# Moving five more transposes from TensorE to DMA in a sparse attention with a dense mixture of experts

## The chip, the cores and the metric

The kernel runs on one core of a Trainium2 chip. The metric is device time in microseconds (us), the median of several runs. A profile of one execution gives the time of every instruction on the engines: TensorE (PE in the profile, PEld its weight loads), VectorE (DVE), ScalarE (ACT), GpSimd (POOL) and SyncE (SP), which only issues DMAs.

## The reference, cut to what matters

Attention comes first: 4 batches of 8 heads, 768 positions, 64 features. Each query sees the keys nearer than 16 positions and 24 block summaries (the maximum of each block of 32 keys, the mean of its values). The result goes into a mixture of 8 experts in which every token takes every expert, weighted by a matrix P that eight rounds of row and column normalization make (a Sinkhorn iteration).

```python
    k_sum = k.reshape(B, H, nb, block, D).max(axis=3)
    v_sum = v.reshape(B, H, nb, block, D).mean(axis=3)
    scores_l = scale * np.matmul(q, k.transpose(0, 1, 3, 2))
    mask_l = np.abs(pos[:, None] - pos[None, :]) < window
    scores_s = scale * np.einsum('bhsd,bhnd->bhsn', q, k_sum)
    scores_s = scores_s + np.log(block)
    # ... softmax over the masked near scores and the summaries together, then
    v_all = np.concatenate([v, v_sum], axis=2)
    return np.matmul(a, v_all).astype(np.float32)
    # ... the experts: x is 3072 x 512, F = 1024
    P = np.exp(logits)
    for _ in range(8):
        P /= P.sum(1, keepdims=True) + 1e-09
        P /= P.sum(0, keepdims=True) + 1e-09
        P *= N / E
    for e in range(E):
        h = np.maximum(x @ w1[e], 0.0)
        ye = h @ w2[e]
        out += P[:, e:e + 1] * ye
```

## The kernel before

The heads are worked on in 16 pairs, four pairs to a batch (`PB` = 4, `NP` = 16). The first four pairs are done in halves; pairs 4 to 15 whole. Every operation of attention and of the first expert is a unit with an engine, an estimated cost, the units it waits for, a priority, and a `lag` by which its result is taken to reach those who wait for it later. A planner written in Python orders the units when the kernel is built, by these estimates. So each engine's queue is fixed before it runs, and the order of one unit changes the order of others. What runs on the chip still waits by semaphores.

Queries and keys arrive with positions along the partitions and are needed with features there. Up to pair 11 TensorE transposes them, six 128x128 blocks each, into a PSUM bank, and ScalarE or VectorE copies them out. From pair 12 on a DMA transposes them:

```python
        def tr(i, z, tag):
            st = at.pop(("st", i, z))
            t = at["t", i, z] = bank(tag, "tkq", BF16)
            for g in range(G):
                if i < PB:
                    for j in range(2):
                        nc.tensor.transpose(t[64 * j:64 * j + 64, g * 128:(g + 1) * 128],
                                            st[:, j, g, :], ident)
                else:
                    nc.tensor.transpose(t[:, g * 128:(g + 1) * 128],
                                        st[:, g, :, :].rearrange("p j d -> p (j d)"), ident)

        def tr_dma(i, z):
            r, st = i % NB, at.pop(("st", i, z))
            nc.sync.dma_start_transpose(out=(kT[r][:], qT[r][:, W:W + S])[z].rearrange("c (g t) -> c g t", g=G),
                                        in_=st[:].rearrange("p g j d -> p (g j d)"))

        def x_dma(i):
            nc.sync.dma_start_transpose(
                out=xT[:, i % PB, i // PB * S:(i // PB + 1) * S].rearrange("c (g t) -> c g t", g=G),
                in_=at.pop(("xs", i, 0))[:].rearrange("p g j d -> p (g j d)"))
# ... (cut)
        def pair_start(i, prio):
            o = i - NB
            war_k = [U.get(("S", o, 0)), U.get(("S", o, 1)), U.get(("km", o))]
            war_q = war_k[:2] + [U.get(("ss", o, 0)), U.get(("ss", o, 1))]
            tag = "m" if i < PB else "a"
            for z in range(2 if i >= PB else 1):
                if i >= 12:
                    U["tr", i, z] = U["kT", i, z] = add("SP", 1.25, lambda z=z: tr_dma(i, z),
                                                        [U["kq"[z], i]] + (war_k, war_q)[z], prio, lag=5.0)
                    continue
                buf = Buffer(tag)
                U["tr", i, z] = add("PE", 0.4, lambda z=z: tr(i, z, tag),
                                    [U["kq"[z], i], U["ident"]] + (war_k, war_q)[z]
                                    + [U["tr", i, 0] if z else U.get(("S", i - 1, 1 if i > PB else 0))],
                                    prio, opens=[buf])
                U["kT", i, z] = add({"ACT": 0.8} if z == 0 else {"ACT": 0.8, "DVE": 0.95},
                                    0, lambda z=z: tr_out(U["kT", i, z].on, i, z), [U["tr", i, z]], prio,
                                    uses=[buf])
```

The four `kT` and `qT` tiles are used in turn (`NB` = 4), so pair 12's transpose overwrites pair 8's. Attention's output goes the same two ways into `xT`, the input of the experts:

```python
        def to_xT(i, h=None):
            t = at.pop(("xs", i, h or 0))
            tx = at["tx", i, h] = bank("a", "tx", FP16)
            for g in range(G if h is None else HG):
                nc.tensor.transpose(tx[:, g * 128:(g + 1) * 128],
                                    t[:, g, :, :].rearrange("p j d -> p (j d)"), ident16)
# ... (cut, in pair_whole)
            if 10 <= i < 15:
                U["xt", i] = U["x", i] = add("SP", 1.25, lambda: x_dma(i), [U["no", i, 0], U["no", i, 1]], prio,
                                             lag=4.5)
            else:
                buf = Buffer("a")
                U["xt", i] = add("PE", 0.35, lambda: to_xT(i), [U["no", i, 0], U["no", i, 1]], prio, opens=[buf])
                U["x", i] = add({"ACT": 0.8, "DVE": 0.9}, 0, lambda: x_out(U["x", i].on, i), [U["xt", i]], prio,
                                uses=[buf])
```

The small copies of neighbouring values (`near_values`, into `Ve`) are issued on the same SyncE queue. GpSimd issues the loads of queries, keys, values and weights. A small copy of one element on GpSimd makes the loads of expert 1's weights wait for the last query transposes:

```python
        def hold():
            for r in range(12 % NB, NB):
                nc.gpsimd.tensor_copy(out=held[0:1, 0:1], in_=qT[r][0:1, W:W + 1])

        last[0] = add("POOL", 0.3, hold, [last[0]] + [U["kT", i, 1] for i in range(12, NP)])
        for i in range(4):
            load(("w1n", i), lambda i=i: load_w1(1, i), 0.85, 1.3)
        load("w2n", lambda: load_w2(1), 0.85, 5.0)
```

The first expert's products (`hidden0` at line 200 and `project0` at line 210) are planned between the pieces of attention, with lower priority, and go on after attention has ended. When the last logits are there, the eight rounds of normalization begin, each of six units on three engines (the loop in `bridge`):

```python
                for eng, us, fn, o, w in (("DVE", 0.62, rows, (), ()), ("POOL", 0.7, by_rows, (), ()),
                                          ("DVE", 0.48, columns, (), ()), ("PE", 0.12, totals, [buf], ()),
                                          ("DVE", 0.2, inverse, (), [buf]), ("POOL", 0.7, by_columns, (), ())):
                    step = add(eng, us, fn, [step], -50.0, opens=o, uses=w, lag=(1.2 if n else 2.0) if fn is columns else 0.0)
```

`totals` is a small matmul by which TensorE sums the columns over the partitions; the profile calls its output "sink". Experts 1 to 7 are computed by a scheme with seven block products in place of eight (the Strassen-Winograd scheme; lines 907 and 913), in a fixed order. The last four pairs of output blocks, A to D, end the kernel. B and D use other PSUM banks (`spare`), and their last sums are split:

```python
            def ahead():
                between(out_acc[:, tb, 0:DH], out_acc[:, tb, 0:DH], out_acc[:, tb, DH:DM])

            def y_half():
                s3 = fast.tile([128, DH], FP32, tag="y3", name="y3", bufs=1)
                nc.scalar.activation(out=s3[:], in_=at(3), func=AF.Copy, scale=P_sb[:, ta, e:e + 1])
                add(tb, 1, 2)
                store(tb, slice(DH, DM))
                nc.vector.scalar_tensor_tensor(
                    out=out_acc[:, tb, 0:DH], in0=at(2), scalar=P_sb[:, tb, 0:1],
                    in1=out_acc[:, tb, 0:DH], op0=ALU.mult, op1=ALU.add)
                nc.gpsimd.tensor_tensor(out=out_acc[:, ta, DH:DM], in0=out_acc[:, ta, DH:DM], in1=s3[:], op=ALU.add)

            def x_half():
                add(ta, 0, 0)
                store(ta, eng=nc.scalar)
                nc.vector.scalar_tensor_tensor(
                    out=out_acc[:, tb, 0:DH], in0=at(1), scalar=P_sb[:, tb, 0:1],
                    in1=out_acc[:, tb, 0:DH], op0=ALU.mult, op1=ALU.subtract)
                store(tb, slice(0, DH))
# ... (cut)
        A, B, C, D = last
        for d, nm in ((A, "q1"), (g, "r21"), (A, "c1"), (q, "ya"), (q, "yb"), (g, "s4"), (B, "q1"), (B, "c1"),
                      (A, "q5"), (A, "v5"), (D, "q1"), (D, "c1"), (B, "q5"), (B, "v5"), (C, "q1"), (C, "c1"),
                      (A, "q6"), (A, "v6"), (D, "q5"), (D, "v5"), (B, "q6"), (B, "v6"), (q, "fin"), (B, "ahead"), (D, "ahead"),
                      (C, "q5"), (C, "v5"), (D, "q6"), (D, "v6")):
            d[nm]()
        for n, d in enumerate(last):
            if n == 1:
                C["q6"]()
                C["v6"]()
            for nm in (("q2", "q4", "q3", "q7", "ya", "yb", "fin"),
                       ("q7", "q3", "y_half", "q2", "q4", "x_half"))[n % 2]:
                d[nm]()
```

`between` is a subtraction, on GpSimd for these four; `add` is one VectorE operation that multiplies a PSUM block by a column of P and adds it to `out_acc`.

## Time and profile before

| | |
|---|---|
| time, median of 3 runs | 677.02 us (675.16 to 677.29) |
| profiled execution, span from first to last instruction | 673.4 us |
| PE busy | 663.9 us (99%), 5111 matmuls |
| PEld busy | 434.8 us (65%) |
| DVE busy | 580.2 us (86%) |
| ACT busy | 402.5 us (60%) |
| POOL busy | 131.5 us (20%) |
| mean TensorE clock granted | 0.999 of full |
| chain that ended last | PE 93%, DVE 4%, DMA, POOL and issue 1% each |

The span is that of one execution, so it differs from the median. Matmuls overlap in TensorE's pipeline: their shown durations add up to more than the time they take, and the distance from one start to the next is the cost. An arrow `<-` in a line of the timeline separates what is written from what is read; in brackets stands the engine's idle time just before, and what ended it. Idle time of an engine that isn't the bottleneck costs nothing. The stages are: start-up to about 20 us, attention mixed with the first expert to about 123 us, the rest of the first expert with the normalization and the first groups of expert 1 to 168.8 us, experts 1 to 7 to the end.

### The profile page before, as it was taken

The page shows a single profiled execution, that of the slowest core. Times are in us where ns is not written, and L with a number is a line of the kernel's source. Part 1 is how long each engine was busy: PE and PEld are TensorE (multiplying, and loading weights), DVE is VectorE, ACT ScalarE, POOL GpSimd, SP SyncE. Part 2 cuts the span into 40 slices and gives each one's busy share as a digit, 9 for nine tenths or more (in the row PEclk, how much of TensorE's full clock was granted, in tenths as well). Part 3 has the DMA queues.
Part 4 walks back from the last instruction along what each step waited for, and adds up shares of the span by engine and source line. Part 5 has one row for each costly group of instructions (what it writes and reads, how often), then busy time and mean ns, then how long its engine had stood idle before and what let it go on. Part 6 is the DMA issues. An engine that isn't in the chain of part 4 may idle for free.

```text
span 673.4 us, 13531 instructions
## 1 busy us (share of the span) xinstructions
PE 663.9 (99%) x5111; PEld 434.8 (65%) x5111; DVE 580.2 (86%) x1433; ACT 402.5 (60%) x783; POOL 131.5 (20%) x177
## 2 busy tenths in 40 slices
PE   8999999999999999999999999999999999999996
PEld 4666655555666666666666666666666666666665
DVE  6878889777799988998899988998899889998885
ACT  4777776565777765555655565555555555556552
POOL 8599622122101010201010010101020101100001
PEclk9999999999999999999999999999999999999999
DMA  9999959000513060311422050405031141201224
GB/s 115 190 147 145 151 85 172 2 1 1 79 11 37 1 79 1 36 14 21 59 22 28 1 78 9 40 1 79 1 33 17 20 60 20 30 0 48 82 91 158
DMA packets 124018, 36.46 MB, mean 54 GB/s; under 512 B 110384, under 2 KB 121136, under 8 KB 123952
## 3 DMA queue, kind: packets, MB, share of 16 engines
q0 software_dynamic: 104672, 26.22, 41.8%
q1 hardware_dynamic: 18464, 8.83, 5.6%
q8 instruction: 40, 0.66, 0.4%
q10 hardware_dynamic: 816, 0.54, 0.2%
q14 instruction: 26, 0.21, 0.1%
HBM read 52.45 MB, written 6.29 MB: 87 GB/s over the span
## 4 chain that ended last, share of the span: by engine, by line
PE 93%; DVE 4%; DMA 1%; POOL 1%; issue 1%; ACT 0%; DVEq 0%; ACTq 0%
PE xy L913 36%; PE pg L907 16%; PE pa L907 11%; PE pb L907 11%; PE hps L200 6%; PE yps L210 6%; PE sg L334 1%; DMA kst<-in_k_dram 1%; DVE hf L857 1%; PE tkq L305 1%; PE vs L342 1%; PE av L406 1%; PE av L412 1%; PE ss L430 1%; PE tx L517 0%
## 5 line engine op out<-in xcount | busy, mean ns | idle before, releaser
L913 PEld LDWEIGHTS <-hf 128*128 128x128 f16 x2352 | 230.1, 98 | 95.6 <-issue 0.5
L913 PE MATMUL xy<-w,hf 128*128 128x256 f16 x1312 | 183.4, 273 | 0.0
L913 PE MATMUL xy<-ws,hf 128*128 128x256 f16 x984 | 147.6, 273 | 0.1
L191 ACT ACTIVATE hf<-pg 128x512 f16<-128x512 f32 x84 | 50.2, 597 | 150.8 <-PE pg L907 150.8
L1049 DVE SCALAR_TENSOR_TENSOR out_acc<-xy,P_sb,out_acc 128x512 f32<-128x512 f32 x164 | 115.1, 744 | 2.1 <-PE xy L913 2.1
L854 DVE TENSOR_TENSOR hf<-hf 128x512 f16<-128x512 f16 x252 | 100.3, 424 | 8.8
L907 PE MATMUL pa<-xT,w 128*128 128x512 f16 x336 | 99.9, 379 | 0.0
L907 PEld LDWEIGHTS <-w 128*128 128x128 f16 x672 | 65.8, 98 | 44.4 <-issue 1.1
L857 DVE TENSOR_TENSOR hf<-pb,c 128x512 f16<-128x512 f32 x84 | 58.1, 692 | 38.5 <-PE pb L907 32.4
L176 POOL DMA_DIRECT2D w<-in_moe_w_dram x56 | 41.7, 754 | 220.6 <-PE pg L907 192.0
L907 PEld LDWEIGHTS <-ws 128*128 128x128 f16 x504 | 49.3, 98 | 25.3
L941 ACT COPY c<-pg 128x512 f32<-128x512 f32 x84 | 49.2, 586 | 22.4 <-PE pg L907 22.4
L857 DVE TENSOR_TENSOR hf<-pg,c 128x512 f16<-128x512 f32 x84 | 57.2, 681 | 0.8 <-PE pg L907 0.8
L926 ACT COPY pg<-pa 128x512 f32<-128x512 f32 x84 | 47.9, 570 | 4.8
L191 ACT ACTIVATE hf<-pa 128x512 f16<-128x512 f32 x84 | 50.6, 602 | 0.0
L907 PE MATMUL pg<-xTs,w 128*128 128x512 f16 x168 | 50.0, 379 | 0.2
L907 PE MATMUL pg<-xT,w 128*128 128x512 f16 x168 | 50.0, 379 | 0.1
L907 PE MATMUL pb<-xT,ws 128*128 128x512 f16 x168 | 50.0, 379 | 0.0
L907 PE MATMUL pb<-xTs,ws 128*128 128x512 f16 x168 | 50.0, 379 | 0.0
L907 PE MATMUL pg<-xTs,ws 128*128 128x512 f16 x168 | 50.0, 379 | 0.0
L934 ACT COPY c<-pb 128x512 f32<-128x512 f32 x84 | 49.8, 592 | 0.0
L200 PE MATMUL hps<-xT,w 128*128 128x384 f16 x256 | 48.6, 326 | 0.0
(141 smaller groups left out, 820.1 us busy)
## 6 DMA issues: line engine op xcount, KB each, us to landing
w<-in_moe_w_dram POOLq DMA_DIRECT2D x8, 1024.0 KB, 8.9
w<-in_moe_w_dram POOLq DMA_DIRECT2D x56, 128.0 KB, 3.5
out_dram<-out_acc SPq DMA_DIRECT2D x20, 256.0 KB, 2.0
qst<-in_q_dram POOLq DMA_DIRECT2D x32, 96.0 KB, 5.7
vx<-in_v_dram POOLq DMA_DIRECT2D x16, 192.0 KB, 6.5
kst<-in_k_dram POOLq DMA_DIRECT2D x24, 96.0 KB, 5.9
w<-in_moe_w_dram POOLq DMA_DIRECT2D x2, 512.0 KB, 8.6
kst<-in_k_dram POOLq DMA_DIRECT2D x4, 192.0 KB, 5.1
```

The costliest lines, as they stand in the source:

```text
L176: nc.gpsimd.dma_start(out=t[:, :, h, :], in_=moe_w1[e].rearrange("(dk p) f -> p dk f", p=128)[:, :, f:f + 128])
L191: nc.scalar.activation(out=out, in_=in_, func=AF.Relu, bias=0.0, scale=1.0)
L200: nc.tensor.matmul(hp[:, 0:n], lhsT=w1s[e][:, dk, 128 * f:128 * (f + 1)], rhs=xT[:, dk, t0:t0 + n], start=(dk == 0), stop=(dk == KD - 1))
L210: nc.tensor.matmul(yp[:], lhsT=h[:, f, c * 128:(c + 1) * 128], rhs=w2s[e][:, f, :], start=(f == 0), stop=(f == KF - 1))
L854: nc.vector.tensor_tensor(out=out, in0=in0, in1=in1, op=ALU.subtract)
L857: nc.vector.tensor_tensor(out=out, in0=in0, in1=in1, op=ALU.add)
L907: nc.tensor.matmul(bank[:], lhsT=w[:, dk, :], rhs=x[:, dk, :], start=start and dk == 0, stop=dk == KH - 1, skip_group_check=True)
L913: nc.tensor.matmul(bank, lhsT=a(f)[:, 128 * c:128 * (c + 1)], rhs=w[:, f, :], start=start and f == 0, stop=f == FH - 1, skip_group_check=True)
L926: nc.scalar.copy(out=B["g"][:], in_=B["a"][:])
L934: nc.scalar.copy(out=B["c5"][:], in_=B["b"][:])
L941: nc.scalar.copy(out=B["c2"][:], in_=B["g"][:])
L1049: nc.vector.scalar_tensor_tensor(out=acc, in0=src, scalar=P_sb[:, t, e:e + 1], in1=acc, op0=ALU.mult, op1=ALU.add)
```

## The change

The keys and queries of pairs 10 and 11 are transposed by DMA in place of TensorE, and so is the output of pair 9. The purpose is to take these transposes off TensorE's queue and the copies behind them off ScalarE and VectorE. The hold on the weight loads follows: it now names all transposes from pair 10 on in the plan, and reads the two tiles written last (those of pairs 14 and 15). The result of the first round's column totals is taken to come 1.4 us later in the plan, so that other work comes ahead of the reciprocal that waits for it in VectorE's queue. And the end of the output pairs B and D is rebuilt: ScalarE's scaling, GpSimd's addition and the subtraction done in advance go; one VectorE sum takes the place of two operations, and the subtraction comes after the second half's sum.

```diff
--- before.py
+++ after.py
@@ -640,7 +640,7 @@
             war_q = war_k[:2] + [U.get(("ss", o, 0)), U.get(("ss", o, 1))]
             tag = "m" if i < PB else "a"
             for z in range(2 if i >= PB else 1):
-                if i >= 12:
+                if i >= 10:
                     U["tr", i, z] = U["kT", i, z] = add("SP", 1.25, lambda z=z: tr_dma(i, z),
                                                         [U["kq"[z], i]] + (war_k, war_q)[z], prio, lag=5.0)
                     continue
@@ -725,7 +725,7 @@
                                    prio, opens=[buf])
                 U["no", i, h] = add("DVE", 0.68, lambda h=h: normalize(i, h),
                                     [U["A", i, h], U.get(("xt", i - 2))], prio, uses=[buf])
-            if 10 <= i < 15:
+            if 9 <= i < 15:
                 U["xt", i] = U["x", i] = add("SP", 1.25, lambda: x_dma(i), [U["no", i, 0], U["no", i, 1]], prio,
                                              lag=4.5)
             else:
@@ -816,10 +816,10 @@
                 expert0(b * S, xs)
                 expert0(b * S + HS, xs)
         def hold():
-            for r in range(12 % NB, NB):
+            for r in range(10 % NB, NB):
                 nc.gpsimd.tensor_copy(out=held[0:1, 0:1], in_=qT[r][0:1, W:W + 1])
 
-        last[0] = add("POOL", 0.3, hold, [last[0]] + [U["kT", i, 1] for i in range(12, NP)])
+        last[0] = add("POOL", 0.3, hold, [last[0]] + [U["kT", i, 1] for i in range(10, NP)])
         for i in range(4):
             load(("w1n", i), lambda i=i: load_w1(1, i), 0.85, 1.3)
         load("w2n", lambda: load_w2(1), 0.85, 5.0)
@@ -1068,18 +1068,11 @@
                     between(out_acc[:, tb, 0:DH], out_acc[:, tb, DH:DM], out_acc[:, tb, 0:DH])
                     store(tb)
 
-            def ahead():
-                between(out_acc[:, tb, 0:DH], out_acc[:, tb, 0:DH], out_acc[:, tb, DH:DM])
-
             def y_half():
-                s3 = fast.tile([128, DH], FP32, tag="y3", name="y3", bufs=1)
-                nc.scalar.activation(out=s3[:], in_=at(3), func=AF.Copy, scale=P_sb[:, ta, e:e + 1])
                 add(tb, 1, 2)
                 store(tb, slice(DH, DM))
-                nc.vector.scalar_tensor_tensor(
-                    out=out_acc[:, tb, 0:DH], in0=at(2), scalar=P_sb[:, tb, 0:1],
-                    in1=out_acc[:, tb, 0:DH], op0=ALU.mult, op1=ALU.add)
-                nc.gpsimd.tensor_tensor(out=out_acc[:, ta, DH:DM], in0=out_acc[:, ta, DH:DM], in1=s3[:], op=ALU.add)
+                between(out_acc[:, tb, 0:DH], out_acc[:, tb, 0:DH], out_acc[:, tb, DH:DM])
+                add(ta, 1, 3)
 
             def x_half():
                 add(ta, 0, 0)
@@ -1089,7 +1082,7 @@
                     in1=out_acc[:, tb, 0:DH], op0=ALU.mult, op1=ALU.subtract)
                 store(tb, slice(0, DH))
 
-            return {f.__name__: f for f in (scale0, q1, c1, q5, v5, q6, v6, q2, q7, q3, q4, ya, yb, fin, ahead, y_half, x_half)}
+            return {f.__name__: f for f in (scale0, q1, c1, q5, v5, q6, v6, q2, q7, q3, q4, ya, yb, fin, y_half, x_half)}
 
         def bridge():
             t = [fps.tile([128, 512], FP32, tag="g", name="allg", bufs=2) for _ in range(2)]
@@ -1129,7 +1122,7 @@
                 for eng, us, fn, o, w in (("DVE", 0.62, rows, (), ()), ("POOL", 0.7, by_rows, (), ()),
                                           ("DVE", 0.48, columns, (), ()), ("PE", 0.12, totals, [buf], ()),
                                           ("DVE", 0.2, inverse, (), [buf]), ("POOL", 0.7, by_columns, (), ())):
-                    step = add(eng, us, fn, [step], -50.0, opens=o, uses=w, lag=(1.2 if n else 2.0) if fn is columns else 0.0)
+                    step = add(eng, us, fn, [step], -50.0, opens=o, uses=w, lag=(1.2 if n else 2.0) if fn is columns else (0.0 if n else 1.4) if fn is totals else 0.0)
 
             X, Wt = {}, {}
             for j in range(2):
@@ -1251,7 +1244,7 @@
         A, B, C, D = last
         for d, nm in ((A, "q1"), (g, "r21"), (A, "c1"), (q, "ya"), (q, "yb"), (g, "s4"), (B, "q1"), (B, "c1"),
                       (A, "q5"), (A, "v5"), (D, "q1"), (D, "c1"), (B, "q5"), (B, "v5"), (C, "q1"), (C, "c1"),
-                      (A, "q6"), (A, "v6"), (D, "q5"), (D, "v5"), (B, "q6"), (B, "v6"), (q, "fin"), (B, "ahead"), (D, "ahead"),
+                      (A, "q6"), (A, "v6"), (D, "q5"), (D, "v5"), (B, "q6"), (B, "v6"), (q, "fin"),
                       (C, "q5"), (C, "v5"), (D, "q6"), (D, "v6")):
             d[nm]()
         for n, d in enumerate(last):
```

## The prediction

> **What bounds the kernel now.** I read the page's slices first, then the list of who waited for whom on TensorE, then the timeline around the places that the change touches. Of the slices of the page (40 slices of 16.8 us; digits are busy tenths):
>
> ```profile
> PE   8999999999999999999999999999999999999996
> DVE  6878889777799988998899988998899889998885
> DMA  9999959000513060311422050405031141201224
> ```
>
> TensorE is at nine tenths or more in every slice but the first and the last; the DMA engines are full in the first 67 us, while attention loads its queries, keys and values, and light afterwards. VectorE is high but has gaps. The list of waits says how little TensorE ever stands still (line, what it waited for: total us, times, longest):
>
> ```profile
> PE sink L1117 <- DVE csum_sb L1112: 0.8, 1, 0.8
> PE ss L430 <- DVE xT L196: 0.5, 1, 0.5
> ```
>
> The other three entries of that list lie in the start-up (1.0, 0.8 and 0.6 us). The chain of work that ended last is 93% TensorE. So the stage from about 20 to 169 us, in which attention is mixed with the first expert's products, lasts as long as TensorE's queue is: the expert's products (lines 200 and 210) are there as filling until 168.8 us, and an instruction taken out of TensorE's queue before that moves everything behind it forward. Work taken from ScalarE or VectorE moves nothing by itself.
>
> The timeline shows what the instructions in question cost (start, duration; the answers' "x6" are six merged instructions):
>
> ```profile
> 76.44 0.50 PE L305 MATMUL tkq<-ident,kst 128*128 128x128 bf16 x6
> 76.78 0.50 PE L305 MATMUL tkq<-ident,qst 128*128 128x128 bf16 x6
> 77.03 0.79 ACT L196 COPY kT<-tkq 128x768 bf16<-128x768 bf16 x1
> 77.20 0.53 PE L342 MATMUL vs<-vx,m_blk 128*64 128x128 bf16 x6
> 77.37 0.56 DVE L196 COPY qT<-tkq 128x768 bf16<-128x768 bf16 x1
> ...
> 81.22 0.50 PE L517 MATMUL tx<-ident,xs 128*128 128x128 f16 x6
> 81.65 0.38 PE L334 MATMUL sg<-qT,kT 64*128 64x160 bf16 x6
> 81.97 0.51 PE L305 MATMUL tkq<-ident,kst 128*128 128x128 bf16 x6
> 82.31 0.50 PE L305 MATMUL tkq<-ident,qst 128*128 128x128 bf16 x6
> 82.65 1.89 PE L210 MATMUL yps<-w,h 128*128 128x512 f16 x8
> ```
>
> These are the last transposes on TensorE for queries and keys (pair 10 at 76.44, pair 11 at 81.97) and the one for pair 9's output (81.22). A duration of 0.50 us contains the pipeline's run-out; what a block takes of the queue is the distance between starts.
>
> **What the Trainium skill says.** "Trace Analysis", section "Identifying the Most-Contended Engine", warns that the busy share of matmuls doesn't tell how near TensorE is to its limit because they are pipelined. Agreed here: six transposes show 0.50 us and take 0.34 (76.44 to 76.78), so I count starts. "VectorE: DVE Perf Modes", "The three transpose paths", has TensorE's transpose end in PSUM, so that a copy follows, and the crossbar DMA's end in SBUF; the trace shows the copies (0.79 us on ScalarE, 0.56 on VectorE). It gives 390 ns for one transpose on TensorE; back to back the trace has 57 (0.34 / 6), and the measurement decides. "DMA: Bandwidth & Descriptors", "Issuing engines are not separate DMA queues", says that DMAs from all queues interleave on the same 16 engines: the transposes added at 60 to 80 us share them with the loads. The table of DMA issues has (KB were not recorded; the number is us to landing)
>
> ```profile
> xT<-xs SPq DMA_TRANSPOSE x5, 4.9
> kT<-kst SPq DMA_TRANSPOSE x4, 5.2
> qT<-qst SPq DMA_TRANSPOSE x4, 3.6
> ```
>
> all after 76 us; beside full loads they may take longer, which no run of before shows.
>
> **The change part by part.**
>
> Transposes. Removed from TensorE: 4 blocks for queries and keys (pairs 10 and 11) and one for an output (pair 9), 30 transposes. Pair 10: 77.20 - 76.44 = 0.76 us. Pair 11: 82.65 - 81.97 = 0.68. Pair 9's output: 81.65 - 81.22 = 0.43. Sum 1.87 us of TensorE's queue, all of it on the path by the argument above. The floor, without the gaps ahead of the next block, is 30 x 57 ns = 1.71 us. Removed too: 2 copies of 0.79 us from ScalarE and 3 of 0.56 from VectorE (3.3 us together), beside other work, so worth nothing in themselves; they help the softmax chain, and free PSUM banks of the ring "a", which five blocks no longer take.
>
> Added: 5 DMA transposes on SyncE's queue, about 1.25 us of issue each (median 1.21 to 1.28 in the trace), 6.3 us in all, between about 60 and 88 us. That queue has room there: between 61.6 and 66.2 and between 68.7 and 73.0 us it issues nothing. Pair 10's keys and queries are issued for loading at 51.8 and 53.5 us and land about 5.8 us later (kst's median), pair 11's at 56.2 and 57.8; the ring entries they overwrite (pairs 6 and 7) are last read by about 62.7 us. So the transposes can be issued from 60 to 65 us, and even with 6 us to landing are done by 75, while pair 10's scores start only at 79.8. Pair 9's output is normalized by 80.7; by DMA it lands near 87, and its logits come after pair 11's output, which landed about 104. No wait follows from either.
>
> Weight loads. Before, GpSimd is held by the last query transpose until 98.0 us, then issues the loads for expert 1. The last transpose is still pair 15's, which waits for pair 11's scores; hence about the same moment, or up to 2 us earlier. First use is at 124.1 us, the last issue at 104.3 plus 8.9 to landing makes 113.2. About 11 us of slack: no effect.
>
> Column totals. TensorE stood 0.78 us before the first totals:
>
> ```profile
> 125.30 0.48 DVE L1112 TENSOR_REDUCE csum_sb<-P_sb 128x8 f32<-128x192 f32 x1
> 125.93 0.36 PE L1117 MATMUL sink<-csum_sb,col_en 128*128 128x8 f32 x2 [0.78 <-DVE csum_sb L1112]
> 128.04 0.20 DVE L1120 RECIPROCAL crec_sb<-sink 128x8 f32<-128x8 f32 x1
> ```
>
> A lag in the planner delays those who wait for a unit. The new 1.4 us is put on the totals, so it moves not them but the reciprocal behind them on VectorE, and with it the rest of the rounds. The old plan shows through: sums' end to totals' 2.0 lag, 0.15 hop, 0.12 for the totals, 0.15 hop make 2.42 us, and the reciprocal came 2.26 us after the sums (125.78 to 128.04). The totals came 2 us sooner than planned, because TensorE was ahead of its plan; hence the wait. The change doesn't address it. But all queues are rebuilt, and VectorE has 3 x 0.56 us less to do before: I count a part of the 0.78 us, -0.3, as a guess. The reciprocal will come 1.4 us later, with weight and input sums for expert 1 done ahead of it. The eighth totals stand at 166.82 with 8 more products (1.73 us) behind them, and P is final at 168.3, first used at 172.4. So 1.4 us fits, by 0.3 us at the totals.
>
> The tail. Of the timeline of the last 6 us:
>
> ```profile
> 668.29 0.73 POOL L1064 TENSOR_TENSOR out_acc<-out_acc 128x256 f32<-128x256 f32 x1 [2.52 <-DVE out_acc L1049]
> 668.31 0.48 DVE L1049 SCALAR_TENSOR_TENSOR out_acc<-py,P_sb,out_acc 128x256 f32<-128x256 f32 x1
> 668.98 0.72 POOL L1082 TENSOR_TENSOR out_acc<-out_acc,y 128x256 f32<-128x256 f32 x1
> 669.49 0.48 DVE L1087 SCALAR_TENSOR_TENSOR out_acc<-px,P_sb,out_acc 128x256 f32<-128x256 f32 x1
> ```
>
> The last VectorE operation ends at 669.97, and the last store follows it. The change keeps four VectorE operations for the last pair of blocks, takes ScalarE's out, and puts a GpSimd subtraction between the first and the last of them. GpSimd does C's subtraction at 668.29 and D's right behind it, 668.98 to 669.70; with 0.1 us to hand over, the last operation starts at about 669.8 in place of 669.49: +0.3 us. What is taken from ScalarE shortens nothing, since VectorE is busy with C's sums until 668.2.
>
> Sum: -1.87 - 0.3 + 0.3 = -1.87 us; 677.02 - 1.87 = 675.15, rounded 675.1.
>
> **The rivals.** (a) The filling runs out. If attention falls behind because a DMA transpose lands late, TensorE would empty its filling before the next batch's inputs are complete. Against: pair 11's output landed near 103.8, and TensorE still had three blocks of earlier projection (about 3 us) after that. For: 1.87 us less work ahead of it. A bubble there would be at most about 1 to 2 us: time 675.5 to 676.5. (b) The transposes slow the loads at 60 to 80 us, or delay the small copies of values that stand behind them in SyncE's queue. Each moves 128 x 768 x 2 bytes = 0.2 MB, so five add 1 MB to a stream of about 142 GB/s: 7 us of that stream. GpSimd waited 5.5 us for old value buffers there (loads are ahead of need), which speaks against; if it came through, pairs 12 to 15 would be later, and the time 676 to 680. (c) The normalization chain becomes the end of the stage: of its 1.73 us of slack at the eighth totals 1.4 are used, and each round can add to it where VectorE's queue is fuller than planned. TensorE would then run out of projection and give back up to 1 us: 676. (d) The rebuilt order happens to remove the waits at 125.15 (0.78) and at 69.84 (0.5) in full: 674.2.
>
> **Range and chances.** The three runs of before lie 675.16 to 677.29, so the median itself may be off by 1 us; with the rivals on one side and (d) on the other I put 672.8 to 677.2. 2% is 13.5 us, seven times the whole of what is moved: faster by over 2% 0.01, slower 0.02 (only if rival (b) upsets the pipeline), within 2% 0.97.
>
> **What would show it.** Right: 96 - 24 = 72 transposes left at line 305, 6 fewer at line 517 (60 left), six DMA transposes each for kT and qT and for xT; the first reciprocal (line 1120) over 3.5 us after its sums in place of 2.26; TensorE's first xy product at about 166.5 in place of 168.68 us; the last VectorE operation 0.3 us further from the last product. Wrong: TensorE waiting for kT, qT or Ve between 60 and 110 us; transposes that take over 10 us to land; a wait at the eighth totals; the first xy product at or after 168.5 us.

## The result, and the profile after

The change made the kernel slower: 681.74 us, median of 4 runs (681.0 to 683.55), against 676.2 us for the kernel before in 4 runs (675.16 to 677.29). The ratio is 1.0086, with an interval of 1.0057 to 1.0114. The prediction of 675.1 us, and its range up to 677.2, missed. The profiled executions span 679.8 us after and 673.4 before.

The slices of the page of after, 17.0 us each (busy tenths; PEclk is TensorE's granted clock in tenths):

```profile
PE   8999979899999999999999999999999999999996
DVE  6878859578599988999889988998899888998885
PEclk9999989899999999999999999999999999999999
DMA  9999999500504022310513050404131041301224
```

Where before had nines, slices 6 and 8 of TensorE (85 to 102 and 119 to 136 us) have a 7 and an 8, and VectorE and the clock dip in the same slices. The DMA engines have no pause at 85 to 102 us, where before had a 5, and there is traffic at 119 to 136 us, where before had a 0. The list of who waited for whom on TensorE (total us, times, longest), after:

```profile
PE av L412 <- DMA Ve<-vx: 4.6, 1, 4.6
PE lp L531 <- DMA xT<-xs: 1.9, 1, 1.9
PE vs L342 <- DMA vx<-in_v_dram: 1.8, 2, 1.1
```

The third lies in the start-up. Two waits are new: for pair 11's copies of values near the window's edge (Ve), and for a transposed output (xT) that the router's logits need. The wait of 0.8 us at the first column totals is gone. TensorE's timeline around the first wait (start, duration, operation; in brackets the idle time before it):

```profile
93.68 0.48 PE L412 MATMUL av<-Ve,Ee 128*128 128x130 bf16 x3 [4.58 <-DMA Ve<-vx]
...
95.26 1.46 PE L200 MATMUL hps<-xT,w 128*128 128x384 f16 x4
...
97.26 0.82 PE L200 MATMUL hps<-xT,w 128*128 128x384 f16 x4
```

Four products with the first expert's weights show 1.46 us right behind the gap and 0.82 two microseconds later. TensorE's busy time and clock in three stretches around the gap (us, busy us and count, granted clock, DMA share, GB/s) say why:

```profile
89.00:93.50 4.50, 0.10 (x4) 1.00 1.87 147
93.50:96.90 3.40, 3.22 (x25) 0.51 1.04 159
96.90:100.00 3.10, 3.10 (x28) 0.98 0.39 73
```

For 3.4 us behind the gap the clock is half. The same happened behind the second wait (127.5 to 131.0 us).

The stage in question is measured from pair 4's first transpose on TensorE to the first xy product. It is 168.68 - 34.66 = 134.0 us before and 175.22 - 34.18 = 141.0 after, +7.0. The sum closes: waits 4.58 + 1.85, less the 0.78 at the totals; two half-clock spells of 3.4 us, worth 1.7 each; less the 1.87 us of transposes taken off: 7.2 us. Before had no wait over 0.8 us and no such spell in that stage.

Why Ve was late is seen in SyncE's timeline of after (start, duration of the issue):

```profile
61.76 1.76 SPq L310 DMA_TRANSPOSE kT<-kst  x1
63.69 1.22 SPq L310 DMA_TRANSPOSE qT<-qst  x1
...
75.30 2.30 SPq L310 DMA_TRANSPOSE kT<-kst  x1
77.76 1.81 SPq L310 DMA_TRANSPOSE qT<-qst  x1
79.74 2.74 SPq L310 DMA_TRANSPOSE kT<-kst  x1
82.65 1.65 SPq L310 DMA_TRANSPOSE qT<-qst  x1
84.41 0.59 SPq L362 DMA_DIRECT2D Ve<-vx  x1
...
86.33 1.08 SPq L364 DMA_DIRECT2D Ve<-vx  x1
```

Pair 11's four Ve copies stand behind the transposes of pairs 12 and 13, whose issue takes 1.65 to 2.74 us each where the plan has 1.25. The last copy, issued at 86.33, lands 7.3 us later, where the plan has 1.9. The page's table of issues (the last number: median us to landing), after:

```profile
Ve<-vx SPq DMA_DIRECT2D x48, 10.2 KB, 5.5
kT<-kst SPq DMA_TRANSPOSE x6, 7.4
qT<-qst SPq DMA_TRANSPOSE x6, 7.9
xT<-xs SPq DMA_TRANSPOSE x6, 6.2
```

Before, these were 5.0, 5.2, 3.6 and 4.9. The first is a median of all 48 copies and hides the moment that counts. Pair 11's four copies alone (issued between 80 and 88 us) take, first before and then after:

```profile
DMA to landing us min/median/max: 4.0/4.7/4.9
DMA to landing us min/median/max: 7.3/7.6/7.8
```

The loads of queries issued between 66 and 90 us, six in each kernel, are slower in the same way, before and after:

```profile
DMA to landing us min/median/max: 4.1/5.8/6.2
DMA to landing us min/median/max: 7.9/10.4/12.6
```

Behind this, the weight loads start late. GpSimd's timeline has, after:

```profile
107.94 0.18 POOL L820 COPY held<-qT 1x1 bf16<-1x1 bf16 x1 [10.93 <-DVE Ee L391]
108.40 5.95 POOL L176 DMA_DIRECT2D w<-in_moe_w_dram  x8 [0.28 <-issue]
```

and before:

```profile
98.00 0.18 POOL L820 COPY held<-qT 1x1 bf16<-1x1 bf16 x1 [7.21 <-DMA qT<-qst]
98.46 5.95 POOL L176 DMA_DIRECT2D w<-in_moe_w_dram  x8 [0.28 <-issue]
```

Eight loads of 128 KB and one of 1 MB follow the hold. Both kernels issue the last output transposed by DMA at the same moment, 115.25 us. Before, the weight loads end at 116.6 us and the output lands after 2.8 us; after, they end at 126.9 and it takes 11.9, and the logits wait for it. At the other end of the kernel, from the start of the last px products to the end of the span, it is 5.5 us before (673.4 - 667.91) and 5.8 after (679.8 - 674.00).

### The profile page after: what moved, and what is told of

The parts are those of the page before. It is cut to its first block, busy times and chain, and to the rows that moved or that the text cites. A ratio compares the mean times of both kernels' runs of the same rounds, so it can differ in the third digit from the quotient of the medians.

```text
span 679.8 us, 13463 instructions
## 1 busy us (share of the span) xinstructions
PE 664.1 (98%) x5081; PEld 433.8 (64%) x5081; DVE 578.4 (85%) x1430; ACT 400.0 (59%) x779; POOL 129.5 (19%) x173
## 4 chain that ended last, share of the span: by engine, by line
PE 91%; DMA 4%; DVE 3%; issue 1%; ACT 0%; POOL 0%; SPq 0%; POOLq 0%; DVEq 0%; ACTq 0%
PE xy L913 36%; PE pg L907 16%; PE pa L907 11%; PE pb L907 11%; PE hps L200 6%; PE yps L210 5%; DMA xT<-xs 2%; PE sg L334 1%; DMA Ve<-vx 1%; DMA vx<-in_v_dram 1%; PE vs L342 1%; PE tkq L305 1%; PE av L412 1%; PE ss L430 0%; PE av L406 0%
```

## The experiments

Theory A: the transposes of pairs 10 and 11, issued while the DMA engines are full with loads, delay SyncE's queue and what shares the DMA engines; TensorE's order is fixed, so it stands still. Rivals: any other order of the queues costs some wait (B, D, R); the output's transposes do it; the new plan of the totals or the tail does it.

All runs in one table; the stage is from pair 4's first transpose to the first xy product in the profiled execution. The last column has TensorE's waits of about 1.4 us or more after the start-up. The profiled execution is one of those that the time is taken from, and executions of one kernel differ, partly by half-clock spells in the start-up: the profiles of e15 and e16 caught their slowest execution (678.72 and 678.0 us). So profiles are compared by their stage.

| run | time, us | ratio to before (interval) | stage, us | waits of TensorE, us |
|---|---|---|---|---|
| before | 676.2 | | 134.0 | none |
| after | 681.74 | 1.0086 (1.0057 to 1.0114) | 141.0 | Ve 4.6, lp 1.9 |
| e1 queries and keys alone | 681.74 | 1.0072 (1.0044 to 1.0100) | 140.8 | Ve 2.9, tx 2.2, ss 1.6 |
| e2 outputs alone | 677.87 | 1.0015 (0.9997 to 1.0033) | 137.1 | tx 1.8 |
| e3 tail and lag alone | 676.5 | 0.9997 (0.9981 to 1.0013) | 137.4 | lp 1.7 |
| e4 Ve of pair 11 from ScalarE | 680.65 | 1.0057 (1.0036 to 1.0078) | 140.0 | sg 2.5, lp 1.7, hps 1.4 |
| e5 idle transposes added | 681.76 | 1.0063 (1.0040 to 1.0086) | 140.7 | lp 3.6 |
| e6 transposes left out | 677.79 | 1.0025 (1.0002 to 1.0048) | 135.9 | hps 2.1 |
| e7 wait filled | 683.92 | 1.0105 (1.0075 to 1.0134) | 137.7 | none |
| e8 loads held less long | 690.51 | 1.0198 (1.0161 to 1.0234) | 149.2 | sg 7.4, Ve 5.0 |
| e9 before again | 677.46 | 0.9998 (0.9979 to 1.0017) | 134.0 | none |
| e10 later landings planned | 686.2 | 1.0134 (1.0091 to 1.0176) | 142.4 | tx 2.7, Ve 1.4, sink 1.4 |
| e11 the same on before | 677.7 | 1.0024 (1.0007 to 1.0042) | 136.8 | none |
| e12 by DMA from pair 13 | 681.39 | 1.0067 (1.0040 to 1.0094) | 139.3 | ss 2.8 |
| e13 = e6, four xs | 676.86 | 1.0015 (1.0003 to 1.0027) | 136.7 | lp 2.1 |
| e14 = e12, four xs | 676.28 | 0.9995 (0.9977 to 1.0012) | 134.9 | none |
| e15 = before, four xs | 675.4 | 0.9990 (0.9979 to 1.0001) | 134.0 | none |
| e16 = e2 + e3, four xs | 674.54 | 0.9976 (0.9963 to 0.9988) | 132.7 | none |
| e17 = after, four xs | 682.12 | 1.0081 (1.0050 to 1.0112) | 140.4 | Ve 5.2 |
| e18 = e16 + pair 11 | 682.38 | 1.0081 (1.0053 to 1.0108) | 140.9 | lp 4.3 |

**The parts alone (e1, e2, e3).** e1 takes only the queries and keys of the change, e2 only the outputs, e3 the lag and the tail:

```diff
-                if i >= 12:                  # e1, and the hold from pair 10
+                if i >= 10:
-            if 10 <= i < 15:                 # e2
+            if 9 <= i < 15:
```

> Only the keys and queries of pairs 10 and 11 go by DMA; pair 9's output, the totals' lag and the tail stay as before. Theory A (SyncE's queue and crowded DMA engines): the copies of neighbouring values of pair 11 again stand behind four transposes, TensorE waits 3 to 5 us for Ve, and the time is 679 to 683 us. Rival B (the lag, the tail or pair 9's output is to blame): no such wait, 674.5 to 676.5 us, the 1.4 us of the removed transposes gained.

> Only pair 9's output goes by DMA. Theory A: no wait for Ve, 0.43 us gained, 675.5 to 676.5 us. Rival B with pair 9's output to blame: a wait of over 2 us appears, 679 us or more.

> The totals' lag and the rebuilt tail alone, all transposes as before. Theory A: no new wait of TensorE in attention; the first reciprocal over 3.5 us after its sums (2.26 before), the tail 0.3 us longer, time 676 to 677.5 us. Rival B with the lag to blame: 679 us or more.

The queries and keys alone have the whole loss, the wait for Ve included. The outputs alone, and the tail with the lag, are within the measurement of before. Yet neither has before's stage: each profile has a wait of 1.7 or 1.8 us and a half-clock spell, though no added query or key transpose. That of e2 is taken up from e12 on. In e3 TensorE waits for pair 11's transposed output, which took 6.7 us to land (4.9 before); up to there e3 has before's order on every engine. So such a wait can come in before's order too, though before's other profiles (before, e9, e15) don't show it.

**The Ve copies from another queue (e4).** Pair 11's four copies leave SyncE's queue; TensorE's and VectorE's orders are those of after.

```diff
-                    nc.sync.dma_start(out=ve[q0 + W:q0 + 2 * W
+                    (nc.scalar if i == 11 else nc.sync).dma_start(out=ve[q0 + W:q0 + 2 * W
```

> The changed kernel with the four copies of pair 11's neighbouring values issued from ScalarE's queue; TensorE's and VectorE's order is the same as in the changed kernel. Theory A1 (place in SyncE's queue): they are issued about 3 us earlier, the wait of 4.6 us falls to 0.5 to 2 us, time 677.5 to 679.5 us. Theory A2 (landing on crowded DMA engines, whoever issues): the wait stays at 4 us or more, time 681 to 682.5 us.

The wait for Ve went; the time is 1 us lower than after's, which the intervals don't tell apart. TensorE's waits in e4:

```profile
PE sg L334 <- ACT er L377: 2.5, 1, 2.5
PE lp L531 <- DMA xT<-xs: 1.7, 1, 1.7
```

ScalarE, which does the exponentials (er), now stands at these DMA issues, and TensorE waits for it instead; the late logits stay. The four copies are issued 2.2 to 3 us earlier than in after, but land no faster:

```profile
DMA to landing us min/median/max: 7.6/7.8/7.9
```

The last lands at 91.72 us, 1.9 earlier. After's TensorE stood ready for it at 89.10 (93.68 - 4.58); e4's is not there before 93.14, because of its own wait and the half clock behind it. So the place in SyncE's queue is worth about 2 us, and the rest is slow landing, whoever issues (A2); the wait went mainly because TensorE came later.

**Crowding alone (e5).** The kernel before, its order kept, with four idle transposes of pairs 10 and 11's staging tiles into tiles nobody reads, ahead of Ve of pairs 9 and 10 in SyncE's queue:

```diff
+            for z in range(2 if i in (9, 10) else 0):
+                nc.sync.dma_start_transpose(out=spare[z]..., in_=at["st", i + 1, z]...)
```

> The kernel before, which transposes pairs 10 and 11 on TensorE, with four more DMA transposes of the same data into tiles that nobody reads, issued from SyncE ahead of the copies of values of pairs 9 and 10; the order of all other queues is that of before. It measures what the transposes cost by crowding alone. Theory A1 (crowding alone does it): TensorE waits for Ve or vx 3 us or more, 679 us or more. Theory A2 (crowding only hurts together with the new order, in which pair 11's values are asked for about 5 us earlier): no wait for Ve over 1 us, 676 to 678 us.

The time is that of after, without one instruction moved on TensorE, VectorE or ScalarE. The wait for Ve expected by A1 did not come; another did, with 6.8 us of half clock (0.83 mean clock from 100 to 120 us). From the list of e5's waits:

```profile
PE lp L534 <- DMA xT<-xs: 3.6, 1, 3.6
```

The wait is for pair 11's output. Its transpose landed 4.3 us after its issue, but was issued at 106.22 us in place of 98.84: SyncE's queue was late. (Not all of this is the crowding's: e5's stage starts 1.8 us later, and its fourth idle transpose waits 1.9 us for the tile that the second still writes.) Pair 11's Ve copies took 7.6 to 8.4 us and landed at 95.45 in place of 87.11; before's order asks for them only at about that time (TensorE uses them from 95.58). So the transposes cost this by what they do to other transfers, without the new order; that the lateness becomes a wait for Ve takes the new order as well, as e6 shows.

**The transposes left out (e6).** The change, its order kept, with the four transposes not issued (pairs 10 and 11 then read stale keys and queries):

```diff
             r, st = i % NB, at.pop(("st", i, z))
+            if i < 12:
+                return
```

> The changed kernel with the four transposes of pairs 10 and 11 left out (those pairs then use old keys and queries); the order of all other queues is that of the changed kernel. Theory A (either form): pair 11's copies are issued about 81.5 us and land in time or nearly, the wait for Ve falls under 1.5 us, 674.5 to 677.5 us. Rival C (the new order by itself, whatever the DMA engines carry): the wait stays over 3 us, 679.5 us or more.

The wait for Ve is gone, the stage falls by 5.1 us, the time by 4. In the same order, pair 11's copies and the loads of queries (in the windows used above) now land as they did before:

```profile
DMA to landing us min/median/max: 3.6/4.3/4.9
DMA to landing us min/median/max: 4.7/5.4/5.6
```

The last copy is issued 1.2 us earlier than in after and lands 4.9 us earlier (88.79 for 93.64), so most of its lateness is slow landing. TensorE uses it at 89.06: the new order leaves 0.3 us of slack, where before's had 6.4 (87.11 to 93.47). With e5 this shows that the four transposes are needed for most of the loss, and enough for one of its size, by another wait. But with 1.87 us less on TensorE the stage should have come under before's 134.0; it is 1.9 us over. TensorE waits behind VectorE, which waits for an xs buffer (the timelines of VectorE and of TensorE in e6):

```profile
110.84 0.56 DVE L512 TENSOR_TENSOR xs<-av,rc 128x384 f16<-128x384 f32 x1 [2.97 <-DMA xT<-xs]
112.95 1.89 PE L200 MATMUL hps<-xT,w 128*128 128x384 f16 x8 [2.12 <-DVE h L193]
```

**The wait filled (e7).** The change with 18 idle matmuls in front of pair 11's first products with Ve, to tell the gap from the slow clock behind it:

```diff
+            if (i, h) == (11, 0):
+                keep_busy(18)
```

> The changed kernel with 18 idle matmuls (some 3.9 us) put into the 4.6 us wait. If TensorE's clock falls because it stood idle: the products behind the wait run at full pace (four products of line 200 in 0.65 to 0.8 us, not 1.46), and about 1.5 us come back: 679.5 to 681 us. If the clock falls for another reason: no change, 681 to 682.5 us.

The time missed what was expected: TensorE waited 2.2 us for pair 1's values in the start-up, which the edit doesn't touch, and 10.2 us of half clock followed there. So pair 11 comes 4.9 us later than in after, and the stretches to look at are those of the idle matmuls and of the products behind them, in e7:

```profile
93.20:97.60 4.40, 4.40 (x27) 1.00 1.06 160
97.60:101.00 3.40, 3.40 (x41) 1.00 0.29 49
```

`hps` takes its normal 0.82 us for four there. The last copy lands at 96.53, 2.7 us after the idle matmuls began, but with TensorE kept busy the clock stays full, to the end of the stage. The stage is 3.3 us shorter than after's; the two half-clock spells that are gone are worth 3.4 us, and the other waits come to about the same.

**The hold (e8).** The change with the weight loads released after pair 14's query:

```diff
-        ... [last[0]] + [U["kT", i, 1] for i in range(10, NP)])
+        ... [last[0]] + [U["kT", i, 1] for i in range(10, NP - 1)])
```

> The changed kernel with the weight loads held only behind pair 14's query transpose, so that they start about 97 in place of 108.4 us. Theory D (weight loads pushed onto the last output transposes make the logits wait 1.9 us): that wait goes, and with it the slow clock behind it, 677.5 to 680 us. Rival: the loads then crowd pair 15's transposes and copies, a wait for Ve or kT takes its place, 681 us or more.

The loads start at 98.31 us, as in before, and the logits' wait is gone, but now the loads overtake pair 15's own transposes (the list of waits in e8):

```profile
PE sg L334 <- DMA qT<-qst: 7.4, 1, 7.4
PE av L412 <- DMA Ve<-vx: 5.0, 1, 5.0
```

Every engine has after's order here; only the loads moved. Pair 15's transposes of keys and queries, issued at 103.8 and 105.9 us, take 10.6 and 13.8 us to land behind them; after's, issued at 103.7 and 105.0, take 2.8 each. So the weight loads do make transposes late, the hold is needed, and it hands every delay of the last query on to the weight loads.

**Before again, and a plan with later landings (e9, e10, e11).** e9 is the kernel before, profiled a second time. e10 and e11 are after and before with the planner's lags nearer to what after's trace shows:

```diff
-  ... prio, lag=5.0)   # transposes of queries and keys
+  ... prio, lag=8.0)
-                                lag=1.9)   # Ve
+                                lag=6.0)
-                                              lag=4.5)   # output transposes
+                                              lag=7.0)
```

> The kernel before, unchanged, for a second profile of it. Theory A (crowding by the added transposes makes the gaps of the changed kernel): no wait of TensorE over 1.5 us between 30 and 170 us, no spell of half clock there, pair 4's first transpose to the first xy product 133.5 to 135 us, time 675 to 678. Rival R (such gaps come and go by chance, and the kernel before has them too): a wait of 1.5 to 3 us for Ve, xT or xs, with a spell of half clock behind it, and a stage of 136 to 138 us.

> The changed kernel with the planner told later landings, nearer to what its trace shows: small copies of values 6.0 us in place of 1.9, transposes of queries and keys 8.0 in place of 5.0, of outputs 7.0 in place of 4.5. Theory A (the loss is TensorE's fixed order meeting transfers that land later than planned): the wait of 4.6 us for pair 11's Ve falls below 1 us, no half clock behind it, the stage falls from 141.0 to 135 to 138 us, and the time to 676 to 679. Rival B (the transfers are late whatever the order; the attention has too little other work to put in their place): waits of 3 us or more in other places, time 680.5 to 683.

> The kernel before with the same later landings in its plan (its own transposes, from pair 12 on, land 3.6 to 5.2 us after issue). Theory A: its landings are near the plan already, so there is nothing to win: 675.5 to 678, stage 133.5 to 136 us. Rival B (any rebuilding of the order costs a wait somewhere): 678 to 681 with a wait of 1.5 us or more.

e9 repeats before (stage 134.0, no new wait), though e3 showed that rival R is not quite excluded. e10 speaks against the part of A that blamed the planner's optimism: the wait for Ve fell to 1.4 us, but three others came, and it is the slowest but one. Told of later landings the planner puts attention later, and TensorE then has nothing left to fill with at its end (from 123.9 us it waits for the last output). In e11 the same costs 1.6 us. So the lateness can't be ordered away by these lags.

**One pair fewer by DMA (e12).**

```diff
-                if i >= 12:                  # before; and the hold from pair 13
+                if i >= 13:
```

> The kernel before with one pair fewer by DMA: queries and keys from pair 13 on, pair 12's back on TensorE, the hold from pair 13. Theory A (transposes beside full loads cost more than the TensorE time they save; those after about 76 us are free): pair 12's lie at the edge, TensorE's 12 transposes come back with about 0.7 us: 676.5 to 678. Rival B (every DMA transpose costs): below 675.5. No wait over 1.5 us for Ve by A.

A's expectation failed: fewer transposes by DMA, and 681.39 us. The wait is again VectorE's for an xs buffer. From the timelines of VectorE and TensorE in e12:

```profile
117.33 0.56 DVE L510 TENSOR_TENSOR xs<-av,rc 128x384 f16<-128x384 f32 x1 [3.15 <-DMA xT<-xs]
...
118.50 0.94 DVE L328 TENSOR_REDUCE ksT<-kT 128x24 bf16<-128x768 bf16 x1
119.50 0.34 PE L430 MATMUL ss<-qT,ksT 64*32 64x384 bf16 x4 [2.84 <-DVE ksT L328]
```

There are two xs buffers, so a pair's normalization waits until the DMA transpose of the pair two before has been read out. VectorE stands there, and all behind it in its queue. e1, e2, e4, e6, e10 and e12 have this wait (longest 3.0, 3.0, 2.4, 3.0, 3.9 and 3.1 us); before has none of 1 us or more.

**Four xs buffers (e13 to e16).** This takes away what makes it wait; the order of every queue stays as it was (e13 against e6, e14 against e12, e15 against before):

```diff
-                                           tag=f"xs{i < PB}", name="xs", bufs=2)
+                                           tag=f"xs{i < PB}", name="xs", bufs=4)
```

> The changed kernel with the four query and key transposes left out, as in e6, and four buffers of xs in place of two; the order of instructions is that of e6. Theory C (the rest of the loss is VectorE's wait for an xs buffer that a DMA transpose still reads): VectorE's wait of 3.0 us and TensorE's wait of 2.1 us for h are gone, no half clock behind it; pair 4's first transpose to the first xy product 132 to 133.5 us in place of 135.9; time 674 to 676. Rival D (any other order than that of before costs some wait): another wait of 1.5 us or more takes its place, stage 135 us or more, time 677 to 679.

> The kernel before with queries and keys by DMA from pair 13 on, as in e12, with four xs buffers; order as in e12. Theory C: VectorE's wait of 3.2 us for xs and TensorE's of 2.8 us for ksT are gone; stage 134.5 to 136 us in place of 139.3; time 676.5 to 679. Rival D: stage 138 us or more, time 680 or more.

> The kernel before with four xs buffers, order unchanged. It has no wait of over 1 us for xs, so by theory C nothing changes in the profiled stage (133.5 to 134.5 us); the time 675.5 to 677, perhaps 0.5 us lower where single executions had such a wait. Rival D expects the same.

> The change without its query and key transposes (outputs from pair 9 by DMA, the tail, the lag on the first totals), with four xs buffers. Theory C: no wait of 1.5 us or more on TensorE after the start-up, stage 133 to 134.5 us, time 675 to 676.8: equal to the kernel before or up to 1.5 us under it. Rival D: stage 136 us or more, time 677.5 to 679.5.

e14 goes from 681.39 to 676.28 us. In the same order the wait is gone (timelines of e14's VectorE and TensorE):

```profile
113.63 0.56 DVE L510 TENSOR_TENSOR xs<-av,rc 128x384 f16<-128x384 f32 x1
114.10 0.94 DVE L328 TENSOR_REDUCE ksT<-kT 128x24 bf16<-128x768 bf16 x1
115.30 0.34 PE L430 MATMUL ss<-qT,ksT 64*32 64x384 bf16 x4
```

Its stage of 134.9 us is before's plus 0.9, near the 0.7 to 0.8 us of pair 12's transposes back on TensorE: e12's loss was the xs buffers. In e13 they took the wait for xs away as well, but the logits' wait for xT came up in its place (2.1 us, with 6.8 us of half clock behind it): there rival D was right. In before the buffers change nothing in the profiled stage, as expected.

e16, the change without its query and key transposes and with four buffers, has no wait over 1 us on TensorE (its list of waits):

```profile
PE idle L555 <- DVE vx L561: 1.0, 1, 1.0
PE vs L342 <- DMA vx<-in_v_dram: 1.0, 1, 1.0
```

Its stage is 1.3 us shorter than before's, which fits pair 9's output off TensorE (0.43) and the totals' wait (0.78), together 1.2. At 674.54 us it beats both kernels: 0.24% under before, interval 0.12 to 0.37%.

**The whole change with four buffers, and half its transposes (e17, e18).** e17 is after with the edit above. e18 is e16 with `if i >= 11` for queries and keys (and the hold from pair 11).

> The whole change with four xs buffers, order as after. Theory A (query and key transposes of pairs 10 and 11 crowd the transfers; the wait for pair 11's Ve and the late weight loads are theirs): the wait of 4 to 5 us for Ve stays, stage 138.5 to 141 us, time 679.5 to 682. Rival C' (the xs buffers are the whole of it): 674 to 676.5 and no Ve wait.

> The change with queries and keys by DMA from pair 11 on (one pair more than before, one fewer than the change), and four xs buffers. Theory A: half the transposes, issued a little later, crowd less: TensorE waits 0 to 3 us for Ve or the last xT; time 675.5 to 679, not under e16's 674.5. Rival E (only the two pairs together are too many; one fits): 673 to 674.5, no wait over 1.5 us.

The buffers don't help the whole change: the wait for Ve stays. And one pair is no half dose. From the lists of waits of e17 and, in the second fence, of e18:

```profile
PE av L412 <- DMA Ve<-vx: 5.2, 1, 5.2
PE lp L531 <- DMA xT<-xs: 1.2, 1, 1.2
```

```profile
PE lp L531 <- DMA xT<-xs: 5.1, 2, 4.3
```

In e18 Ve is in time, but the weight loads start at 106.73 us and the logits wait 4.3 us, with 6.8 us of half clock. Both expectations for e18 were too low.

The logits' wait for the last transposed output goes with the start of the weight loads. It comes in after, e4, e7, e13, e17 and e18: the loads start at 104.6 us or later there, and the output takes 10.5 to 11.9 us to land. Where they start by 103.8 it never comes, and in before, e9 and e3 this output lands within 3.2 us. (e3 and e5 wait for pair 11's output; e10 waits by way of VectorE.) e8 shows the step in between, transposes made late by these loads. The late start itself is not the four transposes' alone: in e6, without them, the loads start at 102.90 us, so 4.4 of after's 9.9 us come with the new order.

## Why the prediction was wrong

**"No wait follows from either."** This step failed. It looked at whether SyncE had room and whether the transposes' own readers would wait, and both were right: TensorE waited for neither kT nor qT of pairs 10 and 11, which were issued from 61.76 us on, about as it said, and landed by 79.0 in place of 75. What stands behind and beside them was not followed, and the slack was read off before's order. Pair 11's Ve copies took 7.3 to 7.8 us to land in place of 4.0 to 4.9, and the rebuilt order asked for them 4.4 us earlier. That was worth 4.6 us of wait and 1.7 of half clock (e1 has this wait, e6 does not).

A misread line helped. "The DMA engines are full in the first 67 us ... and light afterwards": the row has five nines, so they are full to 84 us, and full again in the seventh slice, 101 to 118 us, where the weight loads meet the last outputs. All four new transposes of queries and keys fall into the full part.

**Rival (b) was what happened, and was put aside too cheaply.** It named the delay of "the small copies of values" and 676 to 680 us. Against it stood that GpSimd waited 5.5 us for old value buffers (before's trace has 3.3: 1.10 and 2.23), loads thus being ahead of need. That speaks of the loads of values, not of the small copies made from them, which stand in SyncE's queue. Its own estimate, 7 us of the load stream for five transposes, was the warning, and too small: the last load of queries lands at 93.2 us in after and at 81.9 in e6, 11.3 us for four. The Trainium skill says in "Advanced Engine Details and Errata", section "X-Bar Transpose (TRN2)", that transposes are as fast as regular DMAs. In after the four took 7.1 to 9.3 us to land and the loads of queries beside them 7.9 to 12.6, so by landing they are not slower; but the 11.3 us are twice what their 0.8 MB take at the 142 GB/s of the stream, so in what they cost other transfers they are not like regular DMAs here, and the measurement decides. The 5.2 and 3.6 us read from before were those of a time with lighter load.

**"Weight loads: ... no effect."** Wrong in its timing: the loads started 10 us later, not "up to 2 us earlier", since the last query transpose comes at the end of a delayed chain. The slack of 11 us (from a median of 8.9 us to landing; the last load of that group took 12.3 in before) covered the loads' own readers. It did not cover the last output transposes beside them: 1.85 us of wait, and nearly as much again of half clock.

**The price of a wait.** The prediction counted idle time one for one ("a bubble ... at most about 1 to 2 us"). After the start-up, 14 of the 17 gaps of 1.7 us or more in these profiles bring a half-clock spell, so after's two gaps of 6.4 us together cost about 10. The Trainium skill has the mechanism in "TensorE: Matmul & The Clock Gate", section "What's actually happening": the clock halves after an idle window of about 3.4 us that runs freely. The spells' length agrees, and after's two start 34.1 us apart, ten such windows. But its advice in "Why this matters for your kernels", no gaps over about 3 us, is too mild for this case: 1.85 us was enough, so a window need not be idle throughout.

**The terms of the sum.** -1.87 us for the transposes: the mechanism holds. Pair 12's transposes back on TensorE cost 0.9 us of stage in e14, and e16's stage fits 0.43 for the output. Column totals: -0.3 guessed. The wait of 0.78 is whole in e3, where the lag is the only change ahead of the totals, so the lag doesn't address it, as said. The reordering does: in other runs of after's order it is 0.6 (e6, e17), in e16 and in after itself, whose half clock delays TensorE there, it is gone. The reciprocal came 3.4 us after the sums, against "over 3.5", as seen in after's timelines:

```profile
129.97 0.48 DVE L1105 TENSOR_REDUCE csum_sb<-P_sb 128x8 f32<-128x192 f32 x1
131.55 0.28 PE L1110 MATMUL sink<-csum_sb,col_en 128*128 128x8 f32 x2
133.84 0.20 DVE L1113 RECIPROCAL crec_sb<-sink 128x8 f32<-128x8 f32 x1
```

The tail: +0.3 expected, +0.3 in after's profile, but e3's, with the new tail, is as short as before's (5.2 us from the start of the very last px product), so this is within what profiles differ by. Rivals (a) and (c) did not decide after; a lack of filling was seen only in e10. The prediction's own sign of failure, TensorE waiting for Ve between 60 and 110 us, is the largest wait of after.

## What to carry to other kernels

A DMA taken on to relieve a busy engine is paid in the queue and on the DMA engines it joins: look at what stands behind it and beside it, and take landing times from a moment with the same traffic. A gap of 2 us on TensorE can cost close to 4, so in a fixed order the slack of each transfer against its variation matters more than a microsecond of work saved. Where an engine waits to overwrite a buffer that a DMA still reads, more buffers are the first thing to try: here e14 won back 5 us with them, and the rest of the change (outputs, tail and lag) came out 0.24% ahead of before.

## What was not expected of the hardware

Half-clock spells came in pieces of 3.4 us (6.8 behind some gaps, in e13 after 2.06 us, and 10.2 in e7). They followed gaps of 1.72 us (e3), 1.85 (after) and 2.46 (e4), but not 2.90 us in e1 (at 95.17 us), 2.65 in e10 (at 126.58) or 1.72 in e4 (at 126.96): the length of the gap alone doesn't decide. In the start-up, where TensorE is less dense, less is enough: e16 has 10.2 us of half clock there with no wait over 1.0 us.

The issue of a DMA transpose on SyncE took about 1.2 us at the least, and in after up to 2.89 us (at 91.27) beside full loads, though not each time: three of the first four took 1.22 to 1.24 at 63 to 70 us. The landing says more: 2.8 us with room on the DMA engines, mostly 7 to 12 beside loads. So a queue that seems to have room by its issue times has less of it where the traffic is heavy.
